# A fused attention and gated-convolution kernel: f32 tails, a one-product mask, a shorter closing test and a new plan of all orders

## The chip, the cores and the metric

The kernel runs on one core of a Trainium2 chip. A core has five engines that run side by side, each with its own in-order queue: TensorE (PE in the profile, with its weight loads as PEld), VectorE (DVE), ScalarE (ACT), GpSimd (POOL) and SyncE (SP), which here only issues DMAs. The metric is the device time of one execution in microseconds. Before the change the median of three runs is 197.91 us, with the runs at 193.77, 197.91 and 199.71.

## The reference

Eight batches of eight heads, 576 tokens, 64 elements a head. First an attention with a decay that comes from the input `s`, then a gated linear unit whose gate is a causal convolution of five taps over the tokens:

```
scores = q @ k^T / 8 + min(-(cum_q - cum_k), 0),  cum = cumsum(max(s, 0));  later keys masked
attn   = softmax(scores);   x = attn @ v, heads side by side           # (8, 576, 512)
gate   = sigmoid(sum over k of conv_w[k] * x shifted by 4 - k tokens)
out    = (gate * (x @ w_val)) @ w_out                                  # f32
```

## The kernel before, in words

The unit of work is a pair of heads, n = 4 b + p for batch b and pair p, so there are 32 of them, and later channel block n of the same batch takes the same number. For each batch the kernel does the following.

* Loads. `ld_q`, `ld_k`, `ld_v` and `ld_t` are DMAs that SP issues. `ld_t` brings the last 64 tokens of q and k (the tails) into one tile of 64 + 64 rows. The other q and k of batches 1 to 7 go to f32 staging tiles `qkf` (three of them), v to two tiles `vst`, of which the second lies over the tile `first` that batch 0's q and k use.
* Casts and transposes. `c_q` and `c_k` cast q and k to bf16, `ct` casts the tails. `qt` transposes on TensorE, and `qe` copies the result from PSUM into `QKT`; `tt` and `te` do the same for the tails. `vp` multiplies v by the decay weights (`Vp`).
* Scores and softmax. `s0`, `s1`, `s2` are the products of a pair of heads with keys on the partitions, `s4` those of the last 64 tokens; `e0`, `e1`, `e2`, `e4` are the exponentials on ScalarE (96 of 128x1024, and 11 small). The future keys of the diagonal blocks are masked in one of two ways: `mk`, a select on GpSimd behind `e0`, or, for pairs without `mk`, products on TensorE that add -30000 to the masked scores. Before, that takes two pairs of products (`futA` and `futB`, with the selector `sel`; lines 527 to 534).
* Values. `av0` and `av` are the products with `Vp`, `rec` and `nm` normalise, `xt` transposes, `xe` copies to `xT`.
* The gate. `t1` to `t4` add the four taps to `gp`: on VectorE in one instruction that reads PSUM, or on GpSimd as an addition (line 604), with the product made ahead by `p3` or `p4` (line 591 on GpSimd, line 589 on ScalarE). `th` is the tanh, `val` the product with `w_val`, `glu` the gating.
* The output. `out` is the product with `w_out` in 36 blocks of 128 tokens, four matmuls each (for the last blocks `outa` makes three of the four ahead); `oe` copies PSUM to a staging tile and `st` stores it. Three `oe` are on VectorE, 33 on ScalarE.
* The closing test. `chk0` and `chk` test on GpSimd whether all reciprocals and convolution ratios lie in a safe range, `cnt` counts with a matmul, `cntc` reduces, `flag` loads the count into a register of every engine; a branch (line 727) leads to a slow general path, which does not run here.

All of this is issued from one list, `ORDER`: each word is a step, its engine (S, G, T, A, V for SP, GpSimd, TensorE, ScalarE, VectorE) and the buffers it takes. For one engine the order of the words is the order of its queue. Waits between engines come from the data. `wu` are matmuls whose result nobody reads: they keep TensorE busy.

Of the kernel before, what the change touches and what calls it, by code (L numbers as in the profile page):

```python
# [176 lines left out]
ORDER = """
wu.0:T:0 wu.1:T:1 ld_q.0.0:S ld_s:S ld_k.0.0:S ld_t.0:S c_q.0.0:A ld_q.0.1:S relu:V qt.0.0.q:T:0 ld_k.0.1:S wu.2:T:1
scan:V wu.3:T:2 wu.4:T:1 ld_k.0.2:S c_k.0.0:A wu.5:T:2 wu.6:T:1 qe.0.0.q:A ld_v.0.0:S qt.0.0.k:T:2 wu.7:T:3 wu.8:T:1
qe.0.0.k:V wu.9:T:0 ct.0:A centre:V s0.0:T:4:0 ld_q.0.2:S tt.0:T:0 c_q.0.1:V e0.0:A ld_q.0.3:S wu.10:T:1  # L180
qt.0.1.q:T:2 te.0:V decT:T:3 ld_cw:S qe.0.1.q:A c_k.0.1:V mk.0:G ld_v.0.1:S s1.0:T:6 expw:A s4.0.0:T:4 qt.0.1.k:T:2
c_k.0.2:V e1.0:A s2.0:T:0 qe.0.1.k:V qt.0.2.k:T:3 e4.0.0:A ld_k.0.3:S e2.0:A vp.0.0:V s0.1:T:6:1 ld_q.1.0:S:0
s1.1:T:4 wu.11:T:2 e0.1:A c_q.0.2:V av0.0:T:0 ld_v.0.2:S qe.0.2.k:V av.0:T e1.1:A mk.1:G c_q.0.3:V qt.0.2.q:T:2
wu.12:T:3 rec.0:V s2.1:T:6 nm.0:V qe.0.2.q:A ld_q.1.1:S s4.0.1:T:4 cwT:T:3 e2.1:A xt.0:T:2 vp.0.1:G ld_t.1:S cwc:V
s0.2:T:0:2 e4.0.1:A e0.2:A xe.0:V s1.2:T:6 s4.0.2:T:4 qt.0.3.q:T:3 t1.0:V:0 c_k.0.3:G ld_v.0.3:S e1.2:A av0.1:T:0
vone:G t2.0:V av.1:T qe.0.3.q:A wu.13:T:6 c_q.1.0:G rec.1:V qt.0.3.k:T:7 ld_k.1.0:S:1 e4.0.2:A nm.1:V qe.0.3.k:A
s2.2:T:4 mk.2:G ld_v.1.0:S e2.2:A vp.0.2:V s0.3:T:6:0 s1.3:T:0 wu.14:T:3 ld_k.1.1:S t3.0:V e1.3:A av0.2:T:4 t4.0:V
ld_v.1.3:S c_q.1.1:G av.2:T e0.3:A s2.3:T:0 qt.1.0:T:3 rec.2:V ld_v.1.1:S nm.2:V e2.3:A mk.3:G s4.0.3:T:6 xt.1:T:2
ld_v.1.4:S qt.1.1:T:4 xe.1:A xt.2:T:5 ld_v.1.2:S vp.0.3:G e4.0.3:A qe.1.0:A t1.1:V:1 ld_wv:S:2 t2.1:V xe.2:A ct.1:G
av0.3:T:0 c_k.1.0:G qe.1.1:V av.3:T ld_wo:S:0 tt.1:T:3 rec.3:V s0.4:T:6:1 nm.3:V te.1:A p3.2:G:0 wu.15:T:4 ld_t.2:S  # L190
e0.4:A t3.1:V qt.1.2:T:3 s1.4:T:0 qe.1.2:V s2.4:T:6 e1.4:A c_k.1.1:G wu.16:T:4 t1.2:V:2 e2.4:A p4.2:G:1 t2.2:V
s0.5:T:0:2 ld_q.2:S:1 xt.3:T:3 e0.5:A s1.5:T:6 xe.3:V t3.2:G s2.5:T:4 t4.1:V e2.5:A s0.6:T:0:0 t1.3:V:3 qt.1.3:T:2
mk.5:G e1.5:A wu.17:T:4 wu.18:T:5 qe.1.3:V wu.19:T:4 e0.6:A wu.20:T:5 t2.3:V vp.1.0:G wu.21:T:4 s4.1.3:T:6 s1.6:T:4
vp.1.1:V e4.1.3:A s2.6:T:0 wu.22:T:2 e1.6:A vp.1.2:G av0.4:T:6 t3.3:V av.4:T e2.6:A av0.5:T:4 rec.4:V t4.2:G nm.4:V
av.5:T s0.7:T:2:1 rec.5:V nm.5:V av0.6:T:0 vp.1.3:G e0.7:A s1.7:T:6 cast_wv:V av.6:T e1.7:A p4.3:G:0 s2.7:T:4
xt.5:T:2 e2.7:A rec.6:V nm.6:V ld_k.2:S:2 val.1.0:T:6 t4.3:G val.1.1:T th.1:A:0 xe.5:V ld_v.2.2:S val.3.0:T:4
p3.5:A:1 val.0.0:T:0 glu.1:V cast_wo:G ld_t.3:S xt.6:T:3 th.0:A:1 t1.5:V:1 val.0.1:T th.3:A:2 val.2.0:T:6 glu.0:V
val.3.1:T th.2:A:3 xe.6:V val.2.1:T glu.3:V ct.2:A av0.7:T:0 c_q.2:G av.7:T glu.2:V xt.4:T:4 rec.7:V tt.2:T:5 nm.7:V
# [561 lines left out]
```

## Time and profile before

| what | value |
|---|---|
| runs shown | 193.77, 197.91, 199.71 us |
| profiled execution | span 193.5 us; the page gives no further time for it |
| busy: PE, DVE, ACT, POOL | 173.6, 168.3, 171.1, 164.1 us |
| first exponential starts | 9.55 us |
| last copy to a staging tile ends | 188.87 us |
| HBM read, written | 30.57 MB, 9.44 MB |

The span runs from the first to the last instruction of one execution. An engine is counted as busy while at least one of its instructions runs; on TensorE and ScalarE the instructions overlap a little, so the count times the mean is more than the busy time. The chain of work that ended last is followed back from the last instruction, at each step to what released it. A row of the groups has line, engine, operation, tiles and shapes, count, then busy microseconds, mean nanoseconds of one, and idle time ahead of it.

### The profile page before, as it was taken

How to read it: one execution, taken by the hardware profiler on the slowest of the kernel's cores; microseconds unless marked ns; L12 is line 12 of the kernel's file. 1: busy time of each engine (PE TensorE's matmuls, PEld its weight loads, DVE VectorE, ACT ScalarE, POOL GpSimd, SP SyncE). 2: the span in 40 equal slices, each digit the busy share in tenths (PEclk: the TensorE clock that was granted, in tenths of full speed). 3: DMA queues.
4: the chain of work that ended last, by engine and by line, in shares of the span. 5: the costliest groups of instructions: out<-in, count | busy, mean ns of one | idle time of the engine just before them, and what ended most of it. 6: DMA issues, size and time to landing. Idle time of an engine off the chain costs nothing.

```text
span 193.5 us, 6209 instructions
## 1 busy us (share of the span) xinstructions
PE 173.6 (90%) x2500; PEld 117.6 (61%) x2500; DVE 168.3 (87%) x268; ACT 171.1 (88%) x227; POOL 164.1 (85%) x145
## 2 busy tenths in 40 slices
PE   2988977989989999979989999996999999999980
PEld 0466654667557765747856676674767756765620
DVE  3699899999999899989988999999699999999900
ACT  5399978797999899997999999998899999999650
POOL 6029797999979979999998999986999999699930
PEclk9999999999999999999999999999999999999997
DMA  4998999999599979987999988889742004111353
GB/s 136 264 259 250 238 267 266 321 250 292 162 255 384 228 195 298 338 263 256 248 202 205 346 284 189 241 302 251 163 113 109 4 3 164 58 59 54 124 205 113
DMA packets 62282, 40.44 MB, mean 209 GB/s; under 512 B 47333, under 2 KB 49381, under 8 KB 62250
## 3 DMA queue, kind: packets, MB, share of 16 engines
q1 hardware_dynamic: 62250, 40.01, 74.5%
q8 instruction: 20, 0.33, 0.7%
q14 instruction: 12, 0.10, 0.2%
HBM read 30.57 MB, written 9.44 MB: 207 GB/s over the span
## 4 chain that ended last, share of the span: by engine, by line
PE 34%; DVE 20%; POOL 17%; ACT 10%; issue 8%; DMA 6%; SPq 3%; ACTq 0%; DVEq 0%; POOLq 0%
PE bank L639 7%; PE bank L556 7%; PE bank L622 7%; ACT P L539 7%; POOL gp L604 6%; PE bank L488 6%; DVE gp L602 5%; DMA qkf<-in_k_dram 4%; PE bank L477 3%; DVE gp L600 3%; POOL pr L591 3%; DMA vst<-in_v_dram 3%; DVE Vp L461 3%; DVE glu L630 2%; DVE xn L565 2%
## 5 line engine op out<-in xcount | busy, mean ns | idle before, releaser
L539 ACT ACTIVATE P<-bank 128x1024 bf16<-128x1024 f32 x96 | 94.1, 1044 | 3.8 <-PE bank L488 2.5
L602 DVE SCALAR_TENSOR_TENSOR gp<-bank,cwr,gp 128x574 f32<-128x574 bf16 (+2 forms) x65 | 51.9, 809 | 1.0
L604 POOL TENSOR_TENSOR gp<-gp,pr 128x572 f32<-128x572 f32 (+1 forms) x31 | 43.8, 1415 | 2.3 <-DVE gp L602 1.2
L488 PE MATMUL bank<-QKT 64*128 64x128 bf16 (+4 forms) x576 | 37.4, 240 | 4.3 <-ACT P L539 1.0
L556 PE MATMUL bank<-Vp,P 128*128 128x65 bf16 x960 | 35.6, 194 | 2.7 <-DVE Vp L461 1.2
L556 PEld LDWEIGHTS <-P 128*128 128x128 bf16 x960 | 32.5, 97 | 7.1 <-issue 3.7
L622 PE MATMUL bank<-xT,wv 128*128 128x288 bf16 x256 | 35.7, 286 | 0.8 <-DVE wv L359 0.5
L639 PE MATMUL bank<-wo,glu 128*128 128x512 bf16 x144 | 36.3, 380 | 0.1
L591 POOL TENSOR_TENSOR pr<-xT,cwr 128x572 f32<-128x572 bf16 (+1 forms) x27 | 31.6, 1175 | 1.0 <-DVE xT L359 1.0
L488 PEld LDWEIGHTS <-QKT 64*128 64x128 bf16 x576 | 18.9, 94 | 19.5 <-issue 12.0
L359 ACT COPY QKT<-bank 128x1024 bf16<-128x1024 bf16 (+1 forms) x31 | 28.4, 943 | 2.6 <-PE bank L477 1.6
L545 POOL TENSOR_SCALAR_AFFINE_SELECT P<-P 128x1024 bf16<-128x1024 bf16 x17 | 20.1, 1183 | 12.3 <-ACT P L539 12.3
L622 PEld LDWEIGHTS <-wv 128*128 128x128 bf16 x256 | 23.7, 98 | 9.8 <-issue 2.6
L600 DVE SCALAR_TENSOR_TENSOR gp<-xT,cwr,bank 128x576 f32<-128x576 bf16 x32 | 25.7, 810 | 2.3 <-ACT xT L359 1.4
L565 DVE TENSOR_TENSOR xn<-bank,recs 128x640 bf16<-128x640 f32 x32 | 26.3, 823 | 1.0
L614 ACT ACTIVATE th<-gp,cwr 128x576 f32<-128x576 f32 (+1 forms) x33 | 24.8, 783 | 0.9 <-POOL gp L604 0.5
L630 DVE SCALAR_TENSOR_TENSOR glu<-th,bank 128x576 bf16<-128x576 f32 (+1 forms) x33 | 23.5, 732 | 2.4 <-PE bank L622 0.7
L359 ACT COPY ot<-bank 128x512 f32<-128x512 f32 x33 | 19.8, 604 | 4.2 <-PE bank L639 2.9
L639 PEld LDWEIGHTS <-glu 128*128 128x128 bf16 x144 | 12.4, 98 | 13.5 <-issue 3.0
L461 POOL TENSOR_TENSOR Vp<-vst,w 128x650 bf16<-128x650 f32 x11 | 14.7, 1335 | 1.7 <-DMA vst<-in_v_dram 1.7
L461 POOL TENSOR_TENSOR Vp<-first,w 128x650 bf16<-128x650 f32 x11 | 15.2, 1388 | 0.0
L359 POOL CAST kb<-qkf 128x2048 bf16<-128x2048 f32 (+1 forms) x8 | 13.4, 1675 | 2.0 <-DMA qkf<-in_k_dram 1.9
(82 smaller groups left out, 196.9 us busy)
## 6 DMA issues: line engine op xcount, KB each, us to landing
out_dram<-ot SPq DMA_DIRECT2D x36, 256.0 KB, 2.9
qkf<-in_q_dram SPq DMA_DIRECT2D x12, 512.0 KB, 5.5
qkf<-in_k_dram SPq DMA_DIRECT2D x12, 512.0 KB, 6.0
first<-in_v_dram SPq DMA_DIRECT2D x16, 256.0 KB, 4.9
vst<-in_v_dram SPq DMA_DIRECT2D x12, 256.0 KB, 4.9
vst<-in_v_dram SPq DMA_DIRECT2D x11, 128.0 KB, 4.3
first<-in_q_dram SPq DMA_DIRECT2D x4, 256.0 KB, 4.9
first<-in_k_dram SPq DMA_DIRECT2D x4, 256.0 KB, 4.5
```

The costliest lines, as they stand in the source:

```text
L359: (act.copy if e is act else e.tensor_copy)(dst, src)
L461: e.tensor_tensor(Vps[b % 2][:, :, HP[p]], vslot(b)[:, :, HP[p]], w[:, :, b * 8 + 2 * p:b * 8 + 2 * p + 2].unsqueeze(3).to_broadcast([128, ...
L488: pe.matmul(ps[:, hh, c0:c0 + nq], QKTs[b % 2][r, 1, p, k0:k0 + 128], QKTs[b % 2][r, 0, p, q0:q0 + nq], **kw)
L539: act.activation(out=Pt(n)[:, :, step * 512:(step + 1) * 512], in_=pair((f"s{step}", n)), func=AF.Exp, scale=0.125)
L556: pe.matmul(ps[:, qb * 65:qb * 65 + 65], lhsT, Vps[b % 2][:, kb, 2 * p + hh, :], start=(kb == 0), stop=(kb == qb))
L565: vec.tensor_tensor(xns[b % 2][:, :, p * 128:(p + 1) * 128].rearrange("t g (w d) -> t w g d", w=2), pair(("av", n))[:, :, 0:325].rearrange ...
L591: pool.tensor_tensor(pr, xTs[b % 2][:, c, 4:4 + S - m], r.to_broadcast([128, S - m]), ALU.mult)
L600: vec.scalar_tensor_tensor(gp, xT[:, 3:3 + S], r, xps(n), ALU.mult, ALU.add)
L602: vec.scalar_tensor_tensor(gp[:, m:S], xps(n)[:, 0:S - m], r, gp[:, m:S], ALU.mult, ALU.add)
L604: pool.tensor_tensor(gp[:, m:S], gp[:, m:S], prs[at[f"p{m}", n][0]][:, m:S], ALU.add)
L622: pe.matmul(ps, wv[:, dc, c * 128:(c + 1) * 128], xTs[b % 2][:, dc, 4 + o:4 + o + 288], start=(dc == 0), stop=(dc == 3))
L639: pe.matmul(bank_of(u, i), glu2[:, c, i * 128:i * 128 + 128], wo[:, c, :], start=(c == 0), stop=(c == 3))
```

## The change

* Tails. `ct` is gone, and so are its bf16 tiles. `tt` transposes the f32 tile with an f32 identity of 128x128, and `te` reads f32 from PSUM.
* Mask. One product per head in place of two. The 64 rows of the contraction stand for 128 columns of queries: row i holds, on one side, a large number at key columns from 2i + 2 on and a tiny one at 2i + 1, and on the other side a huge one at query 2i and 1 at query 2i + 1, so that the products are hugely negative where the key is in the future.
* Closing test. `chk0` and `chk` run on VectorE with fewer instructions (a compare, and a compare with a product, each for the early and for the late reciprocals, and two for the ratios), the flags are bf16, and `cnt`, `cntc` and `flag` come at the end of the list.
* Tiles. `qkf` has five slots, of which two lie over `first`; `vst` has two tiles of its own; the bf16 tiles `qkb` are three with planned slots in place of two for each half; `sp`, `cum` and `cw` lie over tiles that are used later.
* A product `p2` for the second tap, so that `t2` can go to GpSimd too.
* `ORDER` is new from the first word to the last: 1097 words where there were 1090.

```diff
-BUFS = {'qkb': 2, 'vst': 2, 'P': 3, 'gp': 4, 'th': 5, 'ot': 4, 'qkf': 3, 'qkw': 2048, 'pr': 2}
+BUFS = {'P': 3, 'gp': 4, 'th': 5, 'ot': 4, 'pr': 2, 'qkf': 5, 'qkb': 3}
...
+ld_q.0.0:S wu.0:T:0 ld_s:S wu.1:T:7 ld_k.0.0:S wu.2:T:0 wu.3:T:7 ld_k.0.1:S wu.4:T:0 ld_t.0:S wu.5:T:7 wu.6:T:0
+wu.7:T:7 ld_cw:S c_q.0.0:G wu.8:T:0 relu:V ld_q.0.2:S wu.9:T:7 scan:V wu.10:T:0 ld_q.0.1:S wu.11:T:7 wu.12:T:0
+wu.13:T:7 ld_q.0.3:S wu.14:T:0 c_k.0.1:A wu.15:T:7 c_k.0.0:V wu.16:T:0 ld_k.0.2:S wu.17:T:7 centre:V wu.18:T:0
+wu.19:T:7 ld_v.0.0:S wu.20:T:2 tt.0:T:0 qt.0.0.q:T:1 qt.0.0.k:T:2 qe.0.0.q:V cwT:T:3 qe.0.0.k:A wu.21:T:7 te.0:V
+wu.22:T:6 ld_k.0.3:S s0.0:T:4:0 cwc:V s1.0:T:0 ld_v.0.1:S e0.0:A decT:T:2 qt.0.1.k:T:6 c_q.0.1:V wu.23:T:7 e1.0:A
...
+val.24.0:T:2 t2.27:G e0.30:A val.24.1:T nm.29:V xt.28:T:0 val.27.0:T:6
+xe.28:V mk.30:G th.27:A:1 glu.24:V s0.31:T:4:0 val.27.1:T e0.31:A t1.28:V:1 p3.28:G:1 s2.30:T:2 xt.29:T:1 e2.30:A
+glu.27:V s1.30:T:4 mk.31:G xe.29:V s2.31:T:6 e1.30:A t4.28:V s1.31:T:2 p3.29:G:0 t1.29:V:2 e1.31:A av0.30:T:4 av.30:T
+t2.28:V t3.29:G e2.31:A val.26.0:T:2 rec.30:V val.26.1:T nm.30:V av0.31:T:6 t3.28:G p4.29:A:0 glu.26:V av.31:T
+xt.30:T:0 rec.31:V t2.29:V out.3.1:T:2 xe.30:A th.28:A:2 nm.31:V p3.30:G:1 out.3.2:T:1 oe.3.1:A:3 t1.30:V:3 xt.31:T:3
+oe.3.2:A:0 t4.29:G st.3.1:S out.3.3:T:2 t2.30:V xe.31:A st.3.2:S out.3.0:T:1 oe.3.3:A:2 t1.31:V:1 t3.30:G p4.30:A:0
+st.3.3:S val.28.0:T:6 t2.31:V oe.3.0:A:3 val.28.1:T val.29.0:T:4 t4.30:G st.3.0:S p3.31:A:1 glu.28:V val.29.1:T
+th.29:A:1 t4.31:V val.30.0:T:0 val.30.1:T th.30:A:2 glu.29:V t3.31:G val.31.0:T:2 glu.30:V val.31.1:T chk:V
+outa.3.8:T:0 th.31.0:A:2 th.31.1:A outa.3.4:T:1 glu.31.0:V glu.31.1:V out.3.4:T out.3.8:T oe.3.4:A:3 outa.3.5:T:2
+oe.3.8:V:2 st.3.4:S out.3.5:T outa.3.7:T:3 st.3.8:S oe.3.5:V:0 out.3.7:T outa.3.6:T:0 st.3.5:S oe.3.7:V:1 out.3.6:T
+cnt:T:1 st.3.7:S oe.3.6:V:3 cntc:V st.3.6:S flag:S
...
+    qkfs = [firstt[:, j * 2048:(j + 1) * 2048] for j in range(2)]
+    qkfs += many("qkf", [128, 2048], FP32, BUFS["qkf"] - 2)
...
     def tail_T(e, b):
         for p in range(4):
-            pe.transpose(bank16[:, at["tt", b][0], p * 128:(p + 1) * 128], tailbs[b % 2][:, p * 128:(p + 1) * 128],
-                         ident)
+            pe.transpose(bank[:, at["tt", b][0], p * 128:(p + 1) * 128], tails[b % 2][:, p * 128:(p + 1) * 128],
+                         identf)
...
+    def future(ps, n, q0):
+        for hh in range(2):
+            r, o = slice(64 * hh, 64 * hh + 64), 128 * hh
+            pe.matmul(ps[:, hh], fut[0][r, o:o + 128], fut[1][r, o + q0:o + 128].unsqueeze(1).to_broadcast(
+                [64, n, 128 - q0]), start=False, stop=True, skip_group_check=True)
...
             if masked:
-                for j in range(2):
-                    for hh in range(2):
-                        r = slice(64 * hh, 64 * hh + 64)
-                        o, fu = ps[:, hh], futB[r]
-                        if j == 0:
-                            o, fu = o.rearrange("k (g q) -> k g q", g=4)[:, :, 0:64], futA[r]
-                        pe.matmul(o, sel[r, j, :], fu, start=False, stop=(j == 1), skip_group_check=True)
+                future(ps, 4, 0)
...
+    def within(e, o, rf):
+        e.tensor_scalar(o, rf, 5e-35, None, ALU.is_ge)
+        e.scalar_tensor_tensor(o, rf, 1.5e31, o, ALU.is_le, ALU.mult)
+
     def check0(e):
...
+        rf = cwr.rearrange("p c k -> p (c k)")
+        e.tensor_tensor(okt, rf, rf, ALU.mult)
+        within(e, ok[:, 0:NE * 10], recs[:, 0:NE].rearrange("p a b c -> p (a b c)"))
+        e.tensor_scalar(ok[:, NS * 10:], okt, 1e12, None, ALU.is_le)
```

How many steps of a kind stand on which engine, before and after:

| step | before | after |
|---|---|---|
| `oe` on ACT, DVE | 33, 3 | 20, 16 |
| `t2`, `t3`, `t4` on POOL | 0, 11, 20 | 7, 14, 17 |
| `p2`, `p3`, `p4` on POOL | 0, 9, 18 | 5, 9, 14 |
| `p2`, `p3`, `p4` on ACT | 0, 2, 2 | 2, 5, 3 |
| `mk` on POOL (the other pairs on PE) | 17 (15) | 16 (16) |
| `te` on ACT, DVE | 2, 6 | 5, 3 |
| `qe` on ACT, DVE | 29, 7 | 25, 11 |
| `xe` on ACT, DVE | 9, 23 | 11, 21 |
| `ct` on ACT, POOL | 2, 6 | none |
| `wu` | 23 | 33 |

More of the change, by code (lines that the diff above doesn't have):

```diff
@@ L195 @@
[L195 to L198, printed above, removed]
-xe.4:A out.0.3:T:6 te.2:A t1.6:V:0 p3.6:G:0 qt.2.1:T:7 oe.0.3:A:0 t1.4:V:3 out.0.2:T:5 st.0.3:S qe.2.1:A c_k.2:G
@@ L304, in main_path @@
              for p in range(4)]
-    vst0 = one.tile([128, NKB, 8, 65], FP32, name="vst")
-    vsts = [vst0, firstt[:, 0:NKB * 520].rearrange("p (i h d) -> p i h d", i=NKB, h=8)][0:BUFS["vst"]]
+    vsts = [one.tile([128, NKB, 8, 65], FP32, name=f"vst{j}") for j in range(2)]
     def v_frame(e, vst):
@@ L376, in decT @@
         for i in range(NKB):
-            pe.transpose(pt[:, i, :], cum[:, WIN[i]:WIN[i] + 128], identf)
+            pe.transpose(pt[:, i, :], cum[:, WIN[i]:WIN[i] + 128], identf[0:64, 0:64])
     def expw(e):
```

247 lines of the change are left out of this document (105 added, 142 removed).

## The prediction, on record before the result

> **What bounds the kernel now.** I read the page first, for the span and the chain that ended last; then busy time by stages, cut where the chain changes engine; then the chain piece by piece.
>
> ```profile
> span 193.5 us, 6209 instructions
> PE 34%; DVE 20%; POOL 17%; ACT 10%; issue 8%; DMA 6%; SPq 3%; ACTq 0%; DVEq 0%; POOLq 0%
> ```
> ```profile
> 14.40:60.00 45.60, 41.10 (x634) 28.70 (x631) 43.91 (x68) 40.90 (x55) 41.55 (x35) 1.00 1.00 260
> 60.00:132.00 72.00, 68.98 (x1065) 48.28 (x1063) 67.13 (x101) 69.74 (x88) 68.40 (x51) 1.00 0.93 265
> 132.00:138.00 6.00, 4.20 (x77) 3.05 (x76) 4.08 (x8) 4.72 (x7) 4.90 (x4) 1.00 1.09 198
> 138.00:166.00 28.00, 27.51 (x445) 19.30 (x440) 26.54 (x45) 27.76 (x38) 26.34 (x23) 1.00 0.26 88
> 166.00:180.50 14.50, 14.11 (x168) 9.47 (x167) 14.03 (x23) 13.55 (x20) 14.01 (x11) 1.00 0.17 65
> 180.50:188.90 8.40, 7.34 (x39) 3.27 (x37) 3.21 (x7) 5.14 (x9) 4.73 (x11) 1.00 0.39 147
> ```
>
> The columns are the stage, its length, the busy time of PE, PEld, DVE, ACT and POOL, the granted clock, the DMA share and GB/s. No engine is the bound. The chain is 34% PE, 20% DVE, 17% POOL and 10% ACT, and in the long stages all four are at 90 to 99%. So moving work between them cannot give much; the stages that can are the head, the hole at 132 and the last 28 us. The chain, in order of time, with start, length and what:
>
> ```profile
> 126.16 6.81 DMA qkf<-in_k_dram
> ...
> 133.10 1.90 POOL kb L359
> 135.04 1.07 PE bank L477 x16
> ...
> 164.94 1.05 ACT P L539
> ...
> 166.05 1.09 POOL P L545
> ...
> 179.10 1.40 POOL gp L604
> 180.59 0.92 POOL ok L651
> ...
> 185.69 0.28 POOL ok L664
> ...
> 186.01 0.36 PE bank L667 x2
> 186.37 1.85 PE bank L639 x8
> ...
> 188.28 0.59 ACT ot L359
> ```
>
> Two things stand out. A load of k, issued at 126.16, holds a cast until 133.1 and the transposes until 135.0: in that hole all four engines fall to 68 to 82%. And from 166.05 (the last select on GpSimd) the chain is GpSimd's queue without a gap, first the taps up to 180.50, then the closing test up to 185.97; `cnt` stands in TensorE's queue ahead of the last two output blocks, so eight matmuls wait for the test.
>
> **The sum, made against the span of 193.5 us.** The page gives no time around it; the runs shown lie 0.3 to 6.2 us above. I carry the ratio over to the median: 197.91 / 193.5 = 1.0228.
>
> *Head.* Before, the first exponential starts at 9.55, 2.5 us after the k transposes start:
>
> ```profile
> 1.42 1.03 PE L572 MATMUL bank<-ident 128*128 128x512 bf16 x2 [1.42 <-POOL ident masks.py:199]
> 3.91 0.62 SPq L414 DMA_DIRECT2D first<-in_q_dram  x1
> 4.92 2.34 PE L572 MATMUL bank<-ident 128*128 128x512 bf16 x5
> 7.05 0.63 PE L477 MATMUL bank<-ident,kb 128*128 128x128 bf16 x4
> 8.27 0.62 ACT L359 CAST tailb<-tail 128x512 bf16<-128x512 f32 x1 [1.29 <-DMA tail<-in_k_dram]
> 9.55 1.02 ACT L539 ACTIVATE P<-bank 128x1024 bf16<-128x1024 f32 x1 [0.67 <-PE bank L488]
> ```
> ```profile
> L359 ACT COPY ot<-bank 128x512 f32<-128x512 f32 x33 | 19.8, 604 | 4.2 <-PE bank L639 2.9 <-issue 1.3
> ```
>
> The new order puts 21 unread matmuls and then `tt.0` ahead of the first `qt` on TensorE. `tt.0` waits for the tail, which was there at 8.27; one more load of k is now issued ahead of it, at about 0.6 us of SP time, so 8.9. With 0.4 us for `tt.0` and the old 2.5 us less 0.6 (transposes at a warm array) the first exponential starts at 11.2, 1.6 late. Behind the waiting `tt.0` stand all transposes and scores. The unread matmuls end between 1.42 + 21 x 0.23 = 6.3 (the pace of the last eight output matmuls, 1.85 / 8) and 1.42 + 21 x 0.47 = 11.3 (2.34 / 5); in the second case the exponential comes at 13.6. In return a cast, a tail cast and four copies of 128x512, 0.6 us each, leave ACT, so it catches up. I take **+1.0**; the ends are 1.6 - 4 x 0.6 = -0.8 and +4.1.
>
> The Trainium skill (TensorE: Matmul & The Clock Gate, Part 1) says that the array runs at half rate until a window of about 3.4 us has been busy, and from then on at full rate. By an estimate from it, 21 unread matmuls without a gap end near 7.6 us, and the head is set by the tail's landing; the 0.47 us pace above agrees with a half-rate array, and no row of before shows a gapless start.
>
> *The hole.* The new order issues the loads further ahead, into five slots. Between `ld_k.7` and `c_k.7`, the pair of the hole, stood 7 steps of ACT and stand 10, some 2 us more, where GpSimd waited 1.62 us (the last field of the row below); the other loads of batches 2 to 7 gain more.
>
> ```profile
> 133.10 1.89 POOL L359 CAST kb<-qkf 128x2048 bf16<-128x2048 f32 x1 [1.62 <-DMA qkf<-in_k_dram]
> ```
>
> ACT was idle for 6.00 - 4.72 = 1.28 us of the hole: **-1.3** (ends 0 and -1.9, the most that any engine, VectorE, lost). What is late next is GpSimd, which casts.
>
> *Middle: work up to the last `mk`.* Rows, and counts from the two orders:
>
> ```profile
> L534 PE MATMUL bank<-futB,sel 64*128 64x512 bf16 x30 | 5.9, 376 | 0.0
> L534 PE MATMUL bank<-futA,sel 64*128 64x256 bf16 x30 | 4.3, 269 | 0.0
> L467 PE MATMUL bank<-ident,tailb 128*128 128x128 bf16 x32 | 3.3, 229 | 0.0
> L377 PE MATMUL bank<-identf,cum 64*128 64x64 f32 x5 | 0.5, 232 | 0.0
> L604 POOL TENSOR_TENSOR gp<-gp,pr 128x572 f32<-128x572 f32 x20 | 28.4, 1423 | 0.8
> L591 POOL TENSOR_TENSOR pr<-xT,cwr 128x572 f32<-128x572 bf16 x18 | 21.4, 1195 | 0.0
> L359 POOL CAST tailb<-tail 128x512 bf16<-128x512 f32 x6 | 4.3, 710 | 0.0
> L602 DVE SCALAR_TENSOR_TENSOR gp<-bank,cwr,gp 128x574 f32<-128x574 bf16 x32 | 25.7, 810 | 0.6
> L359 DVE COPY ot<-bank 128x512 f32<-128x512 f32 x3 | 2.1, 685 | 0.0
> ```
>
> TensorE: the mask of a pair cost (5.9 + 4.3) / 15 = 0.68 us and will cost 5.9 / 15 = 0.39, so 15 x 0.68 - 16 x 0.39 = -3.9. The f32 tail transpose has no row. The nearest is the f32 transpose with 64 columns, 0.10 us busy each, as much as a bf16 one with 128 (3.3 / 32); so the ends are 0 and 32 x 0.10 = +3.3 (double for double the columns), and I take the middle, +1.6. Unread matmuls behind the start: 13 become 7, -6 x 0.23 = -1.4. Together -3.7.
>
> The same skill page (Weight-path perf modes) has a rule against this edit: the fast weight load works for types other than FP32 alone. At its P / 1.2 ns for 128 columns, an estimate of 107 ns, 32 loads cost 3.4 us, about my upper end; by that the sum would be 0.6 later.
>
> GpSimd: seven more additions of taps, 7 x 1.42 = +9.9; one product more, +1.2; six tail casts less, -4.3; two selects less and the moved casts and `vp` close to cancel, so **+6.3** with my count of all steps. VectorE: nine more output copies, 9 x 0.685 = +6.2; five taps less, -4.1; the rest (copies to `QKT` and `xT`, the test) +0.3, so +2.4. ACT: eight output copies less, -4.8, and products, `te` and `xe` that take their place, +0.7 in all.
>
> How much of it reaches the end? I take each engine's share of the chain: -3.7 x 0.34 + 2.4 x 0.20 + 6.3 x 0.17 + 0.7 x 0.10 = **+0.4**. The ends are -3.7 (TensorE alone counts) and +6.3 (GpSimd alone). GpSimd can hide the 6.3 only because it was idle 10.4 us between 14.4 and 166 (the last busy column of the stages: 41.55 + 68.40 + 4.90 + 26.34 of 151.6).
>
> *The last stage.* GpSimd's queue from the last `mk` stays about as long: before, that select and ten steps up to 180.50; now the pair 30 select, one more select, three products and six additions, some 14 us too. Behind it before 8.4 us to the end of the last copy at 188.87. Now:
>
> ```profile
> L614 ACT ACTIVATE th<-gp,cwr 128x288 f32<-128x288 f32 x2 | 1.0, 528 | 0.0
> L630 DVE SCALAR_TENSOR_TENSOR glu<-th,bank 128x288 bf16<-128x288 f32 x2 | 0.9, 455 | 0.0
> ```
>
> two half tanh, 1.06, a half `glu`, 0.46, 14 matmuls at 0.23, 3.2, and a copy on VectorE, 0.69: 5.4, with nothing of the test in front. That is -3.0 at most; VectorE gets four copies and the short test behind its taps, so it may hold the last `glu` up. I take **-2.4** (ends 0 and -3.0; without the wait of `cnt` alone it is some -0.9).
>
> *The end.* `cnt`, `cntc` and `flag` now follow the last block. Every engine loads the count before the branch, in the shadow of the last store; I take **+0.3** (ends 0 and +0.9).
>
> What costs nothing: the loads that SP issues earlier, because SP's time is mostly waiting for output copies:
>
> ```profile
> SPq L647 <- ACT ot L359: 65.4, 26, 10.6
> ```
>
> If a store waits now for a copy behind taps on VectorE, loads behind that store come later; their longer lead covers that.
>
> Sum: +1.0 - 1.3 + 0.4 - 2.4 + 0.3 = -2.0, a span of 191.5, and on the median **195.9 us**, 1.0% less.
>
> **The rivals.**
>
> *GpSimd becomes the bound (slower).* It gets 6.3 us more ahead of the last `mk`, and it casts q and k in the same in-order queue. If it has no idle time where the work falls, casts are late whatever the loads do, and the hole stays. Then -2.0 - 1.1 (its share in the sum) + 6.3 + 1.3 = +4.5: span 198.0, median 202.5, +2.3%. It decides from the point where more than 3.1 us find no idle time. For it: the chain of the last 28 us is GpSimd's already. Against: its 10.4 us idle, and the head, where it waited until 9 us and now has casts to do.
>
> *The new plan fills ACT's gaps (faster).* In 14.4 to 132 ACT was idle for 4.7 + 2.3 = 7.0 us. With TensorE relieved and staging deep, half of it goes: 191.5 - 3.5 = 188.0, median 192.3, -2.8%. For it: the shortage was TensorE's and the loads'; against: VectorE at 43.91 of 45.60 in the first stage, and it gets more.
>
> *More slots bring nothing.* The DMA share is 1.00 and 0.93 up to 132: if the engines are full, a load issued earlier lands no earlier. The hole stays: 192.8, median 197.2.
>
> **How the numbers follow.** Forecast 0.40, slots without effect 0.12, faster 0.25, slower 0.23. A measurement of this kernel tells about 2% from no change, as its runs are 3% apart. The forecast and the third rival are within 2%: 0.52. The forecast's own range is 193 to 199. The range for 8 in 10 reaches into both other cases, half of each left out: 190.5 to 202.5. The ends of the head and of GpSimd's work alone would go to 198 + 2.5 in span, which is why the upper end is the farther one.
>
> **What would show it.** First exponential at 11.2; no wait of a k cast for its load; mask products 0.4 us a pair; GpSimd's idle time between 14.4 and the last `mk` down to 4 us; from its last tap to the last output copy some 5.5 to 6 us. It is wrong if GpSimd's last select comes after 170 (slower) or before 164 (faster), or if the f32 transposes cost more than 0.2 us each.

## The result and the profile after

The changed kernel takes 193.45 us in the median of 17 runs (191.84 to 195.21), the kernel before beside it 195.35 us (193.77 to 199.71). The ratio is 0.9898, with a 95% interval from 0.9868 to 0.9928: 1.0% faster, which is less than the 2% that count as a difference. The profiled execution has a span of 191.6 us and took 193.35 us. Some executions take over 1.5% longer than the fastest of the same kernel and are left out of the ratios; the profiles of `b_newcheck`, `b_cntlast`, `b_chkend`, `a_last_pool` and `a_shift` below come from such executions, so that of these only distances are read, not times from the start.

The page of the changed kernel, span and chain:

```profile
span 191.6 us, 6160 instructions
PE 33%; DVE 21%; ACT 21%; POOL 10%; issue 9%; DMA 3%; SPq 1%; DVEq 0%; ACTq 0%; POOLq 0%
```

Busy time of its engines in the stages that the prediction showed for before (stage, length, PE, PEld, DVE, ACT, POOL, granted clock, DMA share, GB/s):

```profile
14.40:60.00 45.60, 41.86 (x660) 29.65 (x659) 42.08 (x62) 43.76 (x59) 41.74 (x32) 0.96 1.05 272
60.00:132.00 72.00, 68.22 (x1032) 48.52 (x1028) 68.06 (x106) 68.02 (x84) 70.62 (x52) 1.00 0.97 262
132.00:138.00 6.00, 5.92 (x96) 3.91 (x93) 5.85 (x10) 6.00 (x8) 6.00 (x6) 1.00 0.60 147
138.00:166.00 28.00, 27.27 (x425) 18.48 (x422) 26.90 (x44) 26.97 (x37) 27.76 (x23) 1.00 0.26 86
166.00:180.50 14.50, 13.54 (x168) 9.18 (x163) 14.11 (x23) 12.84 (x19) 13.75 (x12) 1.00 0.19 68
180.50:188.90 8.40, 7.02 (x39) 3.44 (x37) 6.62 (x13) 2.98 (x6) 2.02 (x2) 1.00 0.42 157
```

The hole at 132 is gone: GpSimd and ACT are busy all 6.00 us of it, against 4.90 and 4.72. GpSimd's idle time between 14.4 and 166 fell from 10.4 us to 151.6 - (41.74 + 70.62 + 6.00 + 27.76) = 5.5 us (the prediction's sign was 4 up to the last select). Each of the four engines is busy for longer in these 151.6 us than before (PE 143.3 against 141.8, DVE 142.9 against 141.7, ACT 144.8 against 143.1, POOL 146.1 against 141.2, each the sum of four rows). And still the last exponential ends at 173.5 us in both traces. All of the 1.8 us by which the span is shorter (193.48 against 191.65 in the traces) lies behind it. The next table is read from the traces of all kernels of this study; the columns are the end of the last exponential, the further time to the end of the last `glu`, from there to the end of the last copy to a staging tile, from there to the end of the span, and the sum of these three distances.

| kernel | last exponential | to last `glu` | to last copy | to the end | sum of the three |
|---|---|---|---|---|---|
| before | 173.5 | 10.0 | 5.4 | 4.6 | 20.0 |
| after | 173.5 | 10.8 | 3.8 | 3.5 | 18.2 |
| `b_hole` | 173.0 | 10.0 | 5.4 | 5.0 | 20.4 |
| `b_cntlast` | 175.4 | 10.0 | 4.6 | 3.5 | 18.1 |
| `b_newcheck` | 179.7 | 10.2 | 4.6 | 3.5 | 18.3 |
| `b_chkend` | 178.0 | 10.0 | 4.6 | 3.5 | 18.1 |
| `a_oldcheck` | 173.6 | 10.8 | 6.9 | 4.4 | 22.2 |
| `a_cntearly` | 173.8 | 10.8 | 4.3 | 4.7 | 19.8 |
| `a_chkend` | 173.4 | 10.8 | 3.7 | 3.5 | 18.0 |
| `a_twomask` | 173.3 | 10.8 | 3.8 | 5.9 | 20.6 |
| `a_last` | 174.8 | 11.2 | 3.8 | 3.5 | 18.6 |
| `a_last_pool` | 177.6 | 11.2 | 3.8 | 3.5 | 18.6 |
| `a_head` | 175.3 | 10.8 | 3.8 | 3.5 | 18.1 |
| `a_shift` | 177.6 | 10.8 | 3.8 | 3.5 | 18.1 |

Where the count stands at the end of the list, the three distances add up to 18.0 to 18.6 us (`a_twomask` has a reason of its own, below); where it stands ahead of the last blocks, to 19.8 or more. The experiments test that reading.

The rows of the changed kernel's timeline (start, length, engine, line, operation, shapes, count, idle time before and its cause) that answer to the prediction's signs, and two of its groups (count, busy us, mean ns):

```profile
1.44 7.22 PE L556 MATMUL bank<-ident 128*128 128x512 bf16 x21 [1.44 <-POOL ident masks.py:199]
8.86 0.63 PE L454 MATMUL bank<-identf,tail 128*128 128x128 f32 x4 [0.19 <-DMA tail<-in_k_dram]
11.18 2.86 ACT L523 ACTIVATE P<-bank 128x1024 bf16<-128x1024 f32 x3 [0.62 <-PE bank L475]
...
133.03 1.88 POOL L348 CAST qkb<-first 128x2048 bf16<-128x2048 f32 x1
...
168.07 1.09 POOL L529 TENSOR_SCALAR_AFFINE_SELECT P<-P 128x1024 bf16<-128x1024 bf16 x1
170.22 1.09 POOL L529 TENSOR_SCALAR_AFFINE_SELECT P<-P 128x1024 bf16<-128x1024 bf16 x1
...
181.45 1.40 POOL L588 TENSOR_TENSOR gp<-gp,pr 128x573 f32<-128x573 f32 x1 [0.33 <-DVE gp L586]
187.46 0.69 DVE L348 COPY ot<-bank 128x512 f32<-128x512 f32 x1 [0.23 <-PE bank L623]
```
```profile
L486 PE MATMUL bank<-fut,fut 64*128 64x512 bf16 x32 | 6.1, 376 | 0.0
L454 PE MATMUL bank<-identf,tail 128*128 128x128 f32 x32 | 5.1, 282 | 0.2 <-DMA tail<-in_k_dram 0.2
```

The first exponential starts at 11.18 (forecast 11.2). The cast of k at 133.03 has no wait in its last field. The mask of a pair costs 6.1 / 16 = 0.38 us (0.39), an f32 tail transpose 5.1 / 32 = 0.16 us.

### The profile page after: what moved, and what is told of

It is laid out like the page before. It is cut to its first block, busy times and chain, and to the rows that moved or that the text cites. A ratio compares the mean times of both kernels' runs of the same rounds, so it can differ in the third digit from the quotient of the medians.

```text
span 191.6 us, 6160 instructions
## 1 busy us (share of the span) xinstructions
PE 176.6 (92%) x2481; PEld 119.3 (62%) x2481; DVE 172.9 (90%) x279; ACT 166.2 (87%) x214; POOL 166.8 (87%) x136
## 4 chain that ended last, share of the span: by engine, by line
PE 33%; DVE 21%; ACT 21%; POOL 10%; issue 9%; DMA 3%; SPq 1%; DVEq 0%; ACTq 0%; POOLq 0%
ACT P L523 9%; PE bank L540 9%; PE bank L623 6%; POOL gp L588 5%; PE bank L475 5%; PE bank L606 5%; DVE gp L586 4%; PE bank L464 3%; DVE xn L549 3%; ACT QKT L348 3%; DVE QKT L348 3%; DVE glu L614 3%; ACT th L598 3%; DMA tail<-in_k_dram 3%; POOL pr L575 2%
## 5 line engine op out<-in xcount | busy, mean ns | idle before, releaser
L588 POOL TENSOR_TENSOR gp<-gp,pr 128x572 f32<-128x572 f32 (+2 forms) x38 | 56.2, 1486 | 3.7 <-ACT pr L573 0.9
L586 DVE SCALAR_TENSOR_TENSOR gp<-bank,cwr,gp 128x574 f32<-128x574 bf16 (+2 forms) x58 | 46.1, 802 | 0.6
L623 PE MATMUL bank<-wo,glu 128*128 128x512 bf16 x144 | 35.3, 380 | 0.1
L575 POOL TENSOR_TENSOR pr<-xT,cwr 128x572 f32<-128x572 bf16 (+2 forms) x28 | 32.7, 1175 | 1.4 <-DVE xT L348 0.8
L475 PEld LDWEIGHTS <-QKT 64*128 64x128 bf16 x576 | 18.5, 94 | 21.8 <-issue 14.8
L448 POOL TENSOR_TENSOR Vp<-vst,w 128x650 bf16<-128x650 f32 x22 | 29.0, 1335 | 0.5 <-ACT w L369 0.5
L584 DVE SCALAR_TENSOR_TENSOR gp<-xT,cwr,bank 128x576 f32<-128x576 bf16 x32 | 25.7, 809 | 1.3 <-ACT xT L348 0.2
L348 ACT COPY QKT<-bank 128x1024 bf16<-128x1024 bf16 (+1 forms) x25 | 24.9, 1014 | 1.8 <-PE bank L464 1.8
L529 POOL TENSOR_SCALAR_AFFINE_SELECT P<-P 128x1024 bf16<-128x1024 bf16 x16 | 17.5, 1094 | 8.8 <-ACT P L523 8.8
L464 PE MATMUL bank<-ident,qkb 128*128 128x128 bf16 x256 | 19.3, 219 | 0.3 <-DVE gp L586 0.3
L464 PEld LDWEIGHTS <-qkb 128*128 128x128 bf16 x256 | 15.4, 98 | 3.5 <-issue 1.6
L348 POOL CAST qkb<-first 128x2048 bf16<-128x2048 f32 (+2 forms) x11 | 15.5, 1410 | 0.8 <-DMA first<-in_k_dram 0.4
```

The lines of the kernel that those rows point to most:

```text
L348: (act.copy if e is act else e.tensor_copy)(dst, src)
L464: pe.transpose(bank16[:, at["qt", b, p, *w][0], c * 512 + j * 128:c * 512 + (j + 1) * 128], qk_src(which, b, p, j if w else 4 * c + j), ident)
L475: pe.matmul(ps[:, hh, c0:c0 + nq], QKTs[b % 2][r, 1, p, k0:k0 + 128], QKTs[b % 2][r, 0, p, q0:q0 + nq], **kw)
L575: pool.tensor_tensor(pr, xTs[b % 2][:, c, 4:4 + S - m], r.to_broadcast([128, S - m]), ALU.mult)
L586: vec.scalar_tensor_tensor(gp[:, m:S], xps(n)[:, 0:S - m], r, gp[:, m:S], ALU.mult, ALU.add)
L588: pool.tensor_tensor(gp[:, m:S], gp[:, m:S], prs[at[f"p{m}", n][0]][:, m:S], ALU.add)
```

## The experiments

My theory after the result had two parts: the gain is the closing test and the place of its count, and the rest of the new order sums to nothing. The rival was the prediction's own account: hole, mask and order each gain or lose what its terms say. Edits of `ORDER` are shown as the words taken out and put in.

**`b_newcheck`: the kernel before with the new test.**

```
- ... t4.30:G chk0:G ... chk:G ... cnt:T:1 outa.3.6:T:2 cntc:V ... flag:S st.3.6:S st.3.8:S
+ t2.27:V chk0:V ... glu.30:V chk:V ... out.3.8:T cnt:T:1 oe.3.8:A:0 cntc:V st.3.6:S st.3.8:S flag:S
+ check0, check1, count, count_out as in the changed kernel
```

> The kernel before with the closing test of the kernel after and nothing else of the change: on VectorE, its count at the end of the list. Theory 1 (the measured 1% comes from the closing test and what follows it, the new plan of the steps up to the last exponential is worth nothing: there the two traces end at the same 173.5 us): 1.2 to 1.9 us faster than before, ratio 0.990 to 0.994, last output copy at about 188 us. Rival (the gain comes from the plan, the deeper staging and the cheaper mask, and the test only took slack): ratio 0.998 to 1.002.

Measured: ratio 1.001 (0.9962 to 1.0059). Nothing gained, against my theory, although the last stretch of its trace is as short as the changed kernel's (18.3 against 18.2 us). What it gained there it lost earlier: from the end of the last exponential of pair 27 to that of pair 31 its trace has 19.6 us, where before, `b_cntlast` and `b_chkend` have 17.8 each. The first part of the new test stands in that stretch in `b_newcheck` alone; `b_chkend` below shows why that costs.

**`a_oldcheck`: the changed kernel with the old test on GpSimd and the early count.**

```
- st.2.6:S chk0:V ... chk:V ... out.3.6:T cnt:T:1 st.3.7:S oe.3.6:V:3 cntc:V st.3.6:S flag:S
+ t3.31:G chk0:G chk:G ... cnt:T:1 outa.3.7:T:3 ... oe.3.5:V:0 cntc:V ... flag:S st.3.7:S
```

> The kernel after with the closing test of the kernel before: ten steps on GpSimd behind the last tap, its count ahead of the last two output blocks. Theory 1: the 1% is lost again or more, ratio 1.000 to 1.008, because GpSimd's last tap ends at 182.85 here, 2.3 us later than before, and the test of 5.5 us would hold the last eight matmuls up to 188.3. Rival: ratio 0.990 to 0.993.

Measured: ratio 1.0118 (1.0079 to 1.0156), 2.2% behind the changed kernel and more than the theory's 1.000 to 1.008. First and last instruction of the test in its timeline:

```profile
183.03 0.92 POOL L635 TENSOR_SCALAR ok<-recs 128x280 f32<-128x280 f32 x1
...
188.13 0.27 POOL L648 TENSOR_TENSOR ok<-ok,okt 128x40 f32<-128x40 f32 x1
```

The test takes 5.4 us on GpSimd, and in the new order it can begin only at 183.03, because GpSimd's last tap is 2.3 us later than before. The sum of the three distances is 4.0 us more than after (22.2 against 18.2). With the old test and the early count the new order would have been slower than before. The edit moves both, and `a_cntearly` below shows that the early count alone takes some 1.7 us of the 4.0; the new order with the old test and the late count was not run.

**`a_twomask`: the changed kernel with the old two products.**

```
- future(ps, 4, 0)
+ for j in range(2):
+     for hh in range(2):  ...  pe.matmul(o, sel[r, j, :], fu, start=False, stop=(j == 1), ...)
```

> The kernel after with the mask of the kernel before: two pairs of products for a pair of heads, at the places of the new plan. TensorE has 16 x 0.29 us = 4.6 us more. By the share of the chain (a third): 1.5 us slower than the kernel after, ratio 0.996 to 0.999. Rival (TensorE has slack at these places): ratio 0.989 to 0.992. Second rival (TensorE sets the pace, all of it counts): ratio 1.010 or more.

Measured: ratio 1.0051 (1.001 to 1.0092), in none of the three ranges, and in this trace not for the work. The last copy ends at 188.0, where the changed kernel has 188.15, though TensorE has the second products to do again:

```profile
L531 PE MATMUL bank<-futB,sel 64*128 64x512 bf16 x32 | 6.1, 376 | 0.0
L531 PE MATMUL bank<-futA,sel 64*128 64x256 bf16 x32 | 4.4, 269 | 0.0
```

So 4.4 us of TensorE's work reached the last copy with nothing. The loss came behind it: TensorE's branch at 189.17 took 3.70 us in this trace (0.36 us in the changed kernel's), and the closing barrier waited for it. No execution of this kernel has a span under 193.0 us, and the changed kernel's spans lie between 190.1 and 193.5; that fits a branch that is slow each time, but only one execution has a trace.

**`a_shift`: is that branch a matter of the number of instructions in front of it?**

```
- wu.1:T:7 ... wu.3:T:7 ... wu.5:T:7 ... wu.7:T:7
+ sm:T            # 32 products of two columns: pe.matmul(bank[0:2, 7, 0:2], ident[:, 0:2], ident[:, 0:2], ...)
```

> The changed kernel with 32 tiny products of two columns in the head (in place of four of the unread ones), as many instructions more on TensorE as the mask of two products has, and without its work. Theory: TensorE's branch at the end took 3.70 us with the mask of two products, against 0.36, because of where the branch lies in TensorE's stream of instructions; here it takes about 3.7 us again, with the last copy at 188.2 and a span near 193.9, some 1.003 of the time before. Rival: that branch was a matter of that one execution or of the mask; the branch takes 0.36 us, the span is 191.6, 0.99 of the time before.

Measured: 0.9972 (0.9921 to 1.0023). The branch took 0.35 us, so the number alone isn't it, and the theory fell. From the last copy to the end it took 3.5 us. Yet 2.96 us lay outside the span (198.66 against 195.7), and 2.4 to 3.1 in all twelve executions, where the changed kernel has 1.75 (193.35 against 191.6), and 1.7 to 1.9 in all 17. What makes one program pay 3.3 us at TensorE's branch and another 1.2 us outside its span stays open.

**`b_hole`: the kernel before, with the load behind the hole issued 8.5 us earlier.**

```
+ ld_k.7:S:0 st.1.6:S ...
- st.1.8:S ld_k.7:S:0 qt.6.1:T:7
```

> The kernel before with one step moved: the load of k for batch 7 is issued some 8 us earlier, ahead of the store of block 6 of the second group, as soon as its slot is free. The cast then waits for no load and the hole at 132 to 138 us closes. Step of the prediction: 1.3 us less, ratio 0.992 to 0.995. Rival (the hole is made good later by engines that would have waited anyway, and GpSimd casts no sooner): ratio 0.998 to 1.002.

Measured: 0.9972 (0.9928 to 1.0016). The interval holds most of the theory's range of 0.992 to 0.995, and no change at all. The stage and GpSimd's casts in it:

```profile
132.00:138.00 6.00, 4.71 (x86) 3.53 (x83) 4.59 (x9) 5.23 (x7) 6.00 (x6) 1.00 0.64 98
```
```profile
129.57 2.08 POOL L357 CAST qb<-qkf 128x2048 bf16<-128x2048 f32 x1 [2.00 <-DMA qkf<-in_k_dram]
131.62 1.09 POOL L543 TENSOR_SCALAR_AFFINE_SELECT P<-P 128x1024 bf16<-128x1024 bf16 x1
132.66 1.88 POOL L357 CAST kb<-qkf 128x2048 bf16<-128x2048 f32 x1
```

The k cast no longer waits for its load, but it moved from 133.10 to 132.66 only: a wait of 2.00 us (0.65 before) now stands ahead of the q cast in front of it, because the load for that cast, issued at 122.71 instead of 122.64, landed at 129.45 instead of 127.82. So the hole is only half closed (TensorE, VectorE and ScalarE are busy 4.71, 4.59 and 5.23 of its 6.00 us, against 4.20, 4.08 and 4.72). The last exponential comes 0.4 us earlier, the end 0.1. Moving one load earlier made another later; what closing the whole hole is worth, this run does not show.

**`a_last` and `a_last_pool`: work taken off GpSimd.**

```
a_last:       - p3.31:A:1 ... t3.31:G              + t2.31:V t3.31:V
a_last_pool:  the same, and
              - p2.18:G:0 ... t2.18:G              + t3.18:V t2.18:V
              - p2.27:G:1 ... t2.27:G              + t4.27:V t2.27:V
```

> The changed kernel, but the fourth tap of the last tile (its product on ScalarE and its addition on GpSimd) is one instruction on VectorE, put behind t2.31. Theory: GpSimd's last addition, which ended at 182.85 us, sets the end of the kernel; the last tap then ends near 181.3, the first half tanh of the last tile starts 0.9 us earlier (near 182.0 instead of 182.9), the last output copy ends near 187.3 instead of 188.15, and the span is 190.7, some 0.985 of the time before. Rival: the copies of the last tile wait for TensorE's output products of the earlier tiles and for VectorE, which had 0.4 us idle in this stage and gets 0.8 us more; then the last copy stays within 0.3 us of 188.2.

> The same as a_last, and the second tap of tiles 18 and 27 (a product of 1.15 us and an addition of 1.42 us each on GpSimd) is one instruction of 0.81 us on VectorE. Theory: from 60 us on GpSimd sets the pace (98 to 100% busy); it gets 5.1 us less to do before 166 us, VectorE 1.6 us more, so the last exponential ends at 171 to 172.5 instead of 173.5, and the time is 1 to 2.5 us below that of a_last, some 0.975 of the time before. Rival: all four engines are equally full there, and what GpSimd gives up VectorE has to make room for; the last exponential stays within 0.5 us of 173.5 and the time within 0.5 us of a_last.

Measured: `a_last` 0.9904 (0.986 to 0.9949), the same as the changed kernel; `a_last_pool` 1.0003 (0.9958 to 1.0048), 1% worse than `a_last`. My theory, that GpSimd sets the pace, fell both times. In `a_last` the last tap ends earlier, counted from the last exponential (8.4 us behind it instead of 9.4), but the tanh of the last tile, in ACT's timeline, waits for a `glu`:

```profile
182.91 0.78 ACT L597 ACTIVATE th<-gp,cwr 128x576 f32<-128x576 f32 x1 [1.26 <-DVE glu L613]
184.62 0.96 ACT L597 ACTIVATE th<-gp,cwr 128x288 f32<-128x288 f32 x2 [0.93 <-DVE glu L613]
```

`th.28`, `th.30` and `th.31.0` share a buffer, so each waits for the `glu` that reads the one before it, and I had put one more tap on VectorE ahead of `glu.28`. In `a_last_pool` GpSimd gives up 5.1 us of work and VectorE takes 1.6, and the time gets longer than that of `a_last`. Where all four engines are near full, 0.8 us more on VectorE may weigh as much as 2.6 us less on GpSimd; the moved words also change the order of both queues, and no run separates the two.

**`a_cntearly`: the changed kernel with its new test, but the count ahead of the last two blocks.**

```
- out.3.6:T cnt:T:1 st.3.7:S oe.3.6:V:3 cntc:V st.3.6:S flag:S
+ cnt:T:1 outa.3.7:T:3 ... oe.3.5:V:0 cntc:V ... flag:S st.3.7:S
```

> The changed kernel with its test on VectorE, but count, its reduction and its reading put ahead of the last two output blocks, as the kernel before has them. Theory: what the count at the end of the list brought lies behind the last copy: the engines branch after the last store's issue instead of during it. With the early count the last copy stays at 188.2 (0.3 either way), and the time from there to the end is 4.4 to 4.9 us instead of 3.45, a span of 192.6 to 193.2, some 0.995 of the time before. Rival: the length of the end has nothing to do with it and stays at 3.3 to 3.6 us, span 191.3 to 192, 0.99 of the time before.

Measured: 0.9987 (0.9941 to 1.0032): nothing left of the gain. The time from the last copy to the end rises from 3.5 to 4.7 us, and the last copy comes 0.5 us later behind the last `glu`. The last output stores of four kernels (windows of 4 to 5.5 us near the end), in the list of DMA issues (count, KB each, median us from issue to landing), in the order before, `a_cntearly`, after, `b_cntlast`:

```profile
out_dram<-ot SPq DMA_DIRECT2D x2, 256.0 KB, 3.1
```
```profile
out_dram<-ot SPq DMA_DIRECT2D x2, 256.0 KB, 3.7
```
```profile
out_dram<-ot SPq DMA_DIRECT2D x2, 256.0 KB, 2.0
```
```profile
out_dram<-ot SPq DMA_DIRECT2D x3, 256.0 KB, 2.0
```

In each of the first three lines the trace has the landing of one store, in the fourth of two. In before that store is issued at 188.89, more than 1 us after GpSimd, TensorE and VectorE took the branch (187.3 to 187.5); in `a_cntearly` it is issued at 187.86, with ScalarE, GpSimd and TensorE at the branch from 187.7 on. These two land 3.1 and 3.7 us after issue, and such stores of `b_hole` and `a_oldcheck` after 3.5 and 3.2. A store that is only under way when the engines branch is not late: the one issued at 186.30 in before landed after 2.05 us, and in `b_cntlast`, where all engines branch at 190.7 to 190.9, the one issued at 189.96 landed after 2.03. So what comes late are stores issued after other engines have branched, and with the late count there are none.

The traces also show transfers of the instruction queues, one of 16 KB and some of 8 KB. In the four kernels with the early count they fall among the packets of the last stores (in before from 188.45 on, while store packets run to 191.47); in the ten with the late count they begin behind the last of these packets (in the changed kernel at 190.27, behind 189.84). That fits stores held up by the fetching of the instructions behind the branch, but no run separates that cause. That the place of the count decides the length of the end is shown from both sides, by this kernel and by the next.

**`b_cntlast`: the kernel before with three words moved, the old test kept.**

```
- cnt:T:1 outa.3.6:T:2 cntc:V st.3.4:S ... oe.3.8:A:0 flag:S st.3.6:S st.3.8:S
+ outa.3.6:T:2 st.3.4:S ... out.3.8:T cnt:T:1 oe.3.8:A:0 cntc:V st.3.6:S st.3.8:S flag:S
```

> The kernel before, its test still on GpSimd, with count, reduction and reading of the count alone put behind the last output block. Theory: the engines then branch behind the last store's issue, and the time from the last copy to the end falls from 4.6 to 3.5 us; TensorE's products of the last two blocks no longer wait behind the count for GpSimd's test, so the last copy comes 0.3 to 0.9 us earlier; together 1.4 to 2.0 us, 0.990 to 0.993 of the time before. Rival: the end stays at 4.6 us, and only the wait goes: 0.996 to 0.999.

Measured: 0.9881 (0.9837 to 0.9924), as much as the whole change (0.9898). The last copy but one, first in before, then here:

```profile
187.42 0.59 ACT L359 COPY ot<-bank 128x512 f32<-128x512 f32 x1 [1.14 <-PE bank L639]
```
```profile
188.49 0.59 ACT L357 COPY ot<-bank 128x512 f32<-128x512 f32 x1 [0.32 <-PE bank L637]
```

The wait for TensorE, whose products stood behind `cnt` and so behind GpSimd's test, falls from 1.14 to 0.32 us; from the last `glu` to the last copy it is 4.6 us instead of 5.4, and the end falls from 4.6 to 3.5. Together 1.9 us, the whole gain, with the test still on GpSimd.

**`a_head`: a start 2.2 us earlier.**

```
- wu.13 ... wu.19 wu.20 tt.0 qt.0.0.q qt.0.0.k ... te.0 ... s0.0 ... e0.0
+ wu.13 c_k.0.0 centre qt.0.0.q qt.0.0.k qe.0.0.q qe.0.0.k c_k.0.1 ... s0.0 e0.0 ... wu.19 tt.0 te.0 ...
```

> The changed kernel with the transposes of the first pair, their copies, the first scores and the first exponential put ahead of the six last unread products and of the tail's transposes. First exponential near 8.8 to 9.6 instead of 11.18. Theory (as the prediction's sum has it, a later start moves the whole): the last exponential ends 1.5 us earlier, span 190, some 0.982 of the time before. Rival: what comes behind the first stage is set by full engines and by the loads, so the start has slack: at 60 us nothing is left of it, and the time stays within 0.4 us of the changed kernel's, 0.99.

Measured: 0.9917 (0.988 to 0.9955), no better than the changed kernel. ACT's timeline:

```profile
9.02 1.02 ACT L522 ACTIVATE P<-bank 128x1024 bf16<-128x1024 f32 x1
11.60 1.02 ACT L522 ACTIVATE P<-bank 128x1024 bf16<-128x1024 f32 x1 [1.55 <-PE bank L474]
```

The first exponential starts at 9.02 instead of 11.18, the second waits for scores that need the tail, and the last of pair 3 ends at 25.7 us, where the changed kernel has 25.6. The first exponential has slack, and the rival holds for it. A start whose tail also comes earlier was not run.

**`a_chkend` and `b_chkend`: all of the new test where VectorE and GpSimd are idle.**

```
a_chkend:  - st.2.6:S chk0:V ... oe.3.5:V:0 ... oe.3.6:V:3
           + oe.3.8:V:2 chk0:V ... oe.3.5:A:0 ... oe.3.6:A:3
b_chkend:  as b_newcheck, but
           - t2.27:V chk0:V ... glu.30:V chk:V
           + glu.31.1:V chk0:V chk:V
```

> The changed kernel with the first and larger part of its closing test (chk0, four VectorE instructions) moved from 160 us to behind the first output copy of VectorE in the last tile, and two of the last output copies moved from VectorE to ScalarE. Theory: VectorE's instructions from SBUF to SBUF wait for GpSimd's running one; the test took 3.0 us at 160 us in the changed kernel's profile and 4.2 us in that of a_cntearly and a_last, where its first instruction came 0.1 us too late, and there all that follows came 1 us later. Without it at 160 us the last exponential ends at 171.8 to 173.3, and the test costs 1.2 us at most at the end, where GpSimd is idle: last copy at 186.5 to 188, some 0.982 to 0.988 of the time before. Rival: GpSimd is busy without a gap there and sets the pace by itself: the last exponential stays at 173.5 within 0.3, the time at 0.99.

> The kernel before, in its own order, with the changed kernel's short test on VectorE, all of it behind VectorE's last instruction of the last tile (glu.31.1), and count, reduction and reading behind the last output block. Theory: the gain of the change is that of the test and of the place of its count, and b_newcheck gained nothing because the test's first part stood on VectorE among taps, beside a busy GpSimd; here it stands where VectorE is idle and GpSimd has nothing more to do, so the time is that of b_cntlast or 0.2 us less: 0.984 to 0.989 of the time before, last copy 4.5 us behind the last glu, end 3.5 us. Rival: the new order of the rest is worth something too; then this kernel stays at 0.99 or above, clearly behind a_chkend's 0.984, or the test on VectorE costs the same wherever it stands: 1.00.

Measured: `a_chkend` 0.9839 (0.9792 to 0.9887), `b_chkend` 0.9882 (0.9834 to 0.993). First the test's large part in the changed kernel, with GpSimd's instruction beside it; then in `a_last`, where the test starts 0.1 us later; then in `a_chkend`, at the end:

```profile
160.22 0.29 DVE L634 TENSOR_SCALAR ok<-recs 128x280 bf16<-128x280 f32 x1
160.22 2.59 POOL L575 TENSOR_TENSOR pr<-xT,cwr 128x572 f32<-128x572 bf16 x2
160.54 1.27 DVE L635 SCALAR_TENSOR_TENSOR ok<-recs,ok 128x280 bf16<-128x280 f32 x1
161.73 1.11 DVE L641 TENSOR_SCALAR ok<-okt 128x20 bf16<-128x20 f32 x1
```
```profile
160.34 1.30 DVE L633 TENSOR_SCALAR ok<-recs 128x280 bf16<-128x280 f32 x1
160.34 2.30 POOL L574 TENSOR_TENSOR pr<-xT,cwr 128x572 f32<-128x572 bf16 x2
161.67 1.27 DVE L634 SCALAR_TENSOR_TENSOR ok<-recs,ok 128x280 bf16<-128x280 f32 x1
162.87 1.36 DVE L640 TENSOR_SCALAR ok<-okt 128x20 bf16<-128x20 f32 x1
...
167.98 1.40 POOL L587 TENSOR_TENSOR gp<-gp,pr 128x574 f32<-128x574 f32 x1 [1.32 <-DVE recs L544]
```
```profile
185.45 0.30 DVE L633 TENSOR_SCALAR ok<-recs 128x280 bf16<-128x280 f32 x1
185.78 0.45 DVE L634 SCALAR_TENSOR_TENSOR ok<-recs,ok 128x280 bf16<-128x280 f32 x1
186.15 0.17 DVE L640 TENSOR_SCALAR ok<-okt 128x20 bf16<-128x20 f32 x1
```

Twenty elements take 0.17 us when GpSimd is idle and 1.11 or 1.36 us beside it. The Trainium skill (SBUF — State Buffer, section SBUF: two separate sides) says that GpSimd and some VectorE instructions share a pair of ports under an exclusive lock, which the one that starts first holds for its whole instruction. The rows agree: at 160.22 VectorE needed 0.29 us for 280 elements and GpSimd 2.59 us for two products; at 160.34 VectorE needed 1.30 and GpSimd 2.30, the same 0.29 us less. In both, the two engines start within 0.01 us of each other, so far less than the 0.1 us of my expectation decides who waits. In `a_last` the delay goes on to GpSimd, which then waits 1.32 us.

From the end of the last exponential of pair 27 to that of pair 31 it takes 18.5 and 18.6 us in `a_oldcheck` and `a_chkend`, which have no test there, 19.0 in the changed kernel, and 20.2 in `a_cntearly`, `a_last` and `a_twomask`. Part of that is a race that the changed kernel's profiled execution happened to win; it is not all of it, for in `a_head` the step of 280 elements took 0.29 us too, and the stretch 19.9.

In the order of before, the place of the test makes 1.3% (`b_newcheck` 1.001, `b_chkend` 0.9882). In the new order `a_chkend` is the fastest kernel of this study, some 0.6% ahead of the changed kernel by the ratios, but the intervals overlap (0.9887 against 0.9868), so that it beats the change is likely and not shown. It beats the kernel before by 1.6%. My theory had the last exponential move to 171.8 to 173.3 us, and it stayed at 173.4: the rival, that GpSimd sets the pace there by itself, held for that profile, though the time came out in the theory's range.

## Why the prediction was right, and where it was not

The total was right: 195.9 us forecast as 0.990 of the 197.91 then known; measured 0.9898. The span was forecast as 191.5 us and came out as 191.6. The step from span to time was wrong: executions of both kernels lie 1.7 to 2.0 us above their span, not 2.28% of it, so the span of 193.5 stood for about 195.3 us, and the median of 17 runs is 195.35. In the ratio that error cancels. The parts were right in sum up to the last exponential; behind it the errors have opposite signs, -2.4 against a measured -0.7 and +0.3 against -1.1, and to that extent the total is luck.

* **Head, +1.0.** The chain to the first exponential came out as worked (11.18), and its sign was met. But the term did not reach the end: the last exponential moved by 0.0, and a first exponential 2.2 us earlier changed nothing (`a_head`). The step that failed is adding the start to the span. The unread matmuls ended at 1.44 + 7.22 = 8.66 us, between my ends of 6.3 and 11.3. The estimate from the Trainium skill (TensorE: Matmul & The Clock Gate, Part 1) was 7.6; the trace shows the slow pace, one in 0.43 us, to about 6.5 us, 5.1 us after the first of them at 1.44. That is longer than the 3.4 us window that the Trainium skill gives there; the Trainium skill also says in that part that the window runs on its own and does not begin with the kernel.
* **Hole, -1.3.** It closed, as forecast, and no k cast waits there. At first it was worth more than the term: counted by the 96 exponentials of 128x1024, the changed kernel is 1.5 us behind before at the 72nd (135.5 against 134.0) and 2.7 ahead at the 78th, past the hole (144.3 against 147.0), though the two orders place other work differently. By the 96th the two are level again. From 138 to 166 GpSimd is busy for 27.76 of 28.00 us (26.34 before); that GpSimd is what gave the lead back is argued, not shown. One load moved by itself did not close the hole (`b_hole`).
* **Middle, +0.4.** Mask (0.38 us a pair) and f32 transposes (+1.8 us in all against my +1.6) were priced well. Weighting them by shares of the chain gave a small number, and a small number is what there was: undoing the mask moves the last copy by 0.2 us, to the earlier side, in the one trace there is (`a_twomask`). A weight load of the f32 transposes took 0.140 us against 0.102 for bf16, so a load costs 0.04 us more, not the 107 ns that the prediction set beside its sum. GpSimd's load rose by 4.9 us in 14.4 to 166, forecast +6.3. Head, hole and middle gave +0.1 together, and the last exponential moved by 0.0; how the three share in that is not shown.
* **Last stage, -2.4.** Measured: the last copy ends 188.87 - 188.15 = 0.7 us earlier. From GpSimd's last tap to that copy it is 182.85 to 188.15, 5.3 us against 8.4 (my sign said 5.5 to 6): -3.1, more than my term. GpSimd's queue from the select of pair 30 did stay about as long (14.8 us against 14.5). The step that failed is the place of that select: head, hole and middle together had it 0.1 us later, because the +6.3 us of GpSimd's work counted only by its 17% share of the chain, and it starts at 168.07 instead of 166.05. So the test came off the path, and GpSimd's later last tap took 2.3 us of that back. For "the wait of `cnt` alone", -0.9 in the prediction, `b_cntlast` measured 5.4 to 4.6.
* **The end, +0.3.** This is the term that was wrong in sign: 4.6 us became 3.5, -1.1. I had the count "in the shadow of the last store" and charged for what moved behind it. The runs show that an early count is what costs: stores issued after other engines have branched land after 3.1 to 3.7 us instead of 2.0. The trace of before shows its last store landing after 3.1 us where those ahead of it take 2.0 or 2.1, and the sum does not use it.
* **VectorE's "rest (..., the test) +0.3".** The test at 160 us takes 0.30 + 0.29 + 1.27 + 1.11 = 3.0 us, and 4.2 us in the trace of `a_last`, for waiting on GpSimd.
* **Rivals.** GpSimd did get the full queue, 98% to 100% busy from 60 to 166 us, and its very last select, of pair 31, comes at 170.22, which I had named as a sign of "slower"; yet taking work off it gained nothing (`a_last`, `a_last_pool`). The sign was a poor one, since the new order has one more select in the last stage. The plan did not fill ACT's gaps to any profit. "More slots bring nothing" was wrong: the hole closed, and its 0.996 (192.8 / 193.5) lies outside the measured interval. What it says of a load issued earlier, `b_hole` bears out for one pair of loads.

What I would have needed is the table at the top for before alone: 4.6 us from the last copy to the end, for two stores, was the longest stretch of the kernel in which nothing computes.
